# Order of the precomputed weight sums, and the place of one squaring, in a fused attention and MLP kernel

## The chip, the cores and the metric

The kernel runs on one core of a Trainium2 chip. The metric is device time in microseconds (us) of one execution. A core has a matrix engine (PE, with PEld for its weight loads), a vector engine (DVE), a scalar engine (ACT), a general engine (POOL) and a DMA issuer (SP). Each engine takes its own instructions strictly in program order; they meet through semaphores only.

## The reference, cut to what matters

```python
batch, n_heads, seq, head_dim = (8, 12, 448, 64)

def rmsnorm(x, g):
    rms = np.sqrt(np.mean(x * x, axis=-1, keepdims=True) + 1e-06)
    return x / rms * g
q_n, k_n = (rmsnorm(q, g_q), rmsnorm(k, g_k))
scores = scale * np.matmul(q_n, k_n.transpose(0, 1, 3, 2))
...
attn = np.exp(scores)
...
return np.matmul(attn, v)

# then, per batch: d_model 768, inner width 3072
xn = (x - mu) / np.sqrt(var + 1e-06) * g_ln
ch = np.maximum(xn @ w_ch1, 0.0) @ w_ch2
return x + ch
```

## The kernel before, in words

**Tiling.** Heads go in pairs, six pairs to a batch, 48 in all (pair numbers p). Pairs are prepared in units (u) of up to two pairs; from unit 4 on a unit is two pairs of one batch. For each pair the attention has seven steps (i = 0 to 6). In step i the code first emits whatever the preparation plan has put there, then `scores(p, i)` (L405, in step 6 L411 for both pairs at once; PE writes a block of scores into a PSUM bank `psS`, ACT takes exp of it into `E`, L421), then `values(p - 1, i)` (L458 and L460, products of the E of the pair before with the values; step 1 does two of them). There are two `psS` banks and a third one, so that a score block can be written when the exp three blocks back is done. After the last product of a pair `evac_o` (L473 to L480, DVE) divides by the row sums and frees `oA` and `oB`; the next pair's products need these.

**Two streams in one.** `run_rest` goes over the batches. The MLP of batch b is a list of chunks, and after each half chunk `upto` emits so many attention steps of batch b+1 that both end together. Batch 0 has its own form, `first_mlp`: up products, and then 24 down chunks (`psC`, L728), six banks of four chunks, each ended by an `add` (L755, DVE). In it the attention is done with the last 11 chunks still to go; after each of those one piece of the layer norm of batch 1 follows: statistics, `norm` of two token tiles (L662, DVE), and their transposes by DMA into `xnT` (L688, issued by SP).

**The MLP from batch 1 on** (`mlp_group`) multiplies two token tiles by w2 with seven block products instead of eight. Products take w2 itself or sums of its four blocks b11, b12, b21, b22: T1 = b12 - b11, T2 = b22 - T1, T4 = b21 - T2, and T3 = b12 - b22, which is written over b12. T1, T2 and T4 lie in `w2s`. Product "7" needs T3 after nine up chunks and product "1" of the first group; "6", "5" and "4" need T2, T1 and T4 later, "4" (T4) last. `weight_sums` (L761) makes each sum in four DVE subtractions of 1152 columns, T1, T2 and T4 of one quarter after one another, then those of the next; the four of T3 are in `last`. `run_rest` gives out one of these 16 subtractions after each chunk: in batch 0 when fewer than nine chunks are left (`left < 9`), the rest in batch 1, one a chunk from its first.

**The preparation of a unit** (`pieces`) is a set of lettered operations that `PLAN` puts into steps, counted from four pairs ahead of the unit's first pair: a, the square of the keys on ACT (L259, `khl<-k`); i, keys by the gains on POOL (L279); c, the square of the queries on ACT (L259, `qn<-q`), the first reader of the loaded queries; d and e, the row sums of the two squares on DVE (L265); j, the keys in fp16 on ACT (L287); k, their remainder on DVE (L290); g, the root (L268, L269); l, the scaled queries on DVE (L83); m, their copy; x, y, Y, transposes by DMA on SP. Units 10 to 24, fifteen of them, follow `PLAN`; here they are called steady units. The others have places of their own. The query buffer is one of a ring of three; when a k or an l has freed one, the load of a later unit goes into it (L146 and L154, SP), behind what SP has in its queue.

Of the kernel before, what the change touches and what calls it, by code (L numbers as in the profile page):

```python
# [51 lines left out]
NAMES = {8: ["bai", "d", "c", "e", "j", "k", "gz", "l", "m"],  # L52
         9: ["bai", "d", "c", "j", "k", "e", "gz", "l", "m"]}
W2_AT = 47, 71
PLAN = ((0, "bai"), (1, "dc"), (3, "j"), (5, "k"), (6, "e"), (7, "g"), (8, "l"), (9, "m"),
        (12, "z"), (15, "x"), (16, "y"), (18, "Y"))
LOAD_AT = 3, 1
LN_EXP_SET = 6
# [33 lines left out]
class _Fast:  # L92
# [447 lines left out]
    def attention(self):  # L540
# [3 lines left out]
        for u in range(4, nu):  # L544
            p, m = UNIT_PAIR[u], UNITS[u][2]
            if u == 4:
                continue
            plan = [(7 * (p - 4) + x, y) for x, y in PLAN]
            if u in EARLY:
# [208 lines left out]
    def weight_sums(self):  # L758

        nc, w2, w2s = self.nc, self.sh.w2, self.w2s  # L760
        sub = lambda out, a, b: nc.vector.tensor_tensor(out=out, in0=a, in1=b, op=ALU.subtract)  # L761
        ops = []
        for c in range(4):
            f, f2 = slice(3 * c, 3 * c + 3), slice(HALF + 3 * c, HALF + 3 * c + 3)
            b11, b12, b21, b22 = w2[:, f, 0:HCOL], w2[:, f, HCOL:DM], w2[:, f2, 0:HCOL], w2[:, f2, HCOL:DM]
            t1, t2, t4 = (w2s[:, i, f] for i in range(3))
            ops += [lambda a=a: sub(*a) for a in ((t1, b12, b11), (t2, b22, t1), (t4, b21, t2))]
        last = [lambda f=slice(3 * c, 3 * c + 3), f2=slice(HALF + 3 * c, HALF + 3 * c + 3): sub(
            w2[:, f, HCOL:DM], w2[:, f, HCOL:DM], w2[:, f2, HCOL:DM]) for c in range(4)]
        return ops, last  # L770

    def mlp_group(self, b, tiles, end, before=(), after=()):

# [186 lines left out]
    def upto(self, target):  # L960
        while self.pos < min(target, len(self.steps)):
            for call in self.steps[self.pos]:
                call()
            self.pos += 1
# [8 lines left out]
    def run_rest(self):  # L973
        steps, mark, upto = self.steps, self.mark, self.upto
        for b in range(B):
            tail = TAIL[b]
            chunks = list(self.mlp_chunks(b))
            total = sum(c for c, _ in chunks)
            if b + 1 == B:
                for i, (_, emit) in enumerate(chunks):  # L980
                    if i == len(chunks) - 55:
                        self.tc.mark_branch_hint_location("general", "LikelyTaken", [ENG.PE, ENG.DVE, ENG.SP, ENG.Activation, ENG.Pool])
                    for call in emit if isinstance(emit, list) else [emit]:
                        call()
                    if i in FLAG_AT:
                        self.flag(FLAG_AT.index(i))
                break
            start, goal = self.pos, mark[b + 1]
            done, items = 0.0, None
            if b == 0:  # L990
                ops, last = self.weight_sums()
            elif b == 1:
                ops += last
            left = sum(c > 0 for c, _ in chunks)
            for cost, emit in chunks:
                if not cost:
                    emit()
                    continue
                for i, call in enumerate(emit):
                    call()  # L1000
                    if i + 1 < len(emit):
                        upto(int(min(goal, start + (goal - start) * (done + cost / 2) / (total - 960 * tail))))
                left -= 1
                if (left < 9 if b == 0 else b == 1) and ops:
                    ops.pop(0)()
                done += cost
                upto(int(min(goal, start + (goal - start) * done / (total - 960 * tail))))
                if self.pos >= goal:
                    if items is None:
                        items = self.ln_list(b + 1)  # L1010
                        for u, (x, _, _) in enumerate(UNITS):
                            if x == b + 2 and self.late_v(u):
                                self.ln[f"Z{u}"] = self.prep_ops(u)["z"]
                                items.append(f"Z{u}")
                    if items and (items[0][0] != "X" or left <= DOWN):
                        x = items.pop(0)
                        self.ln[x]()
            for x in items:
                self.ln[x]()
            if b + 2 == B:  # L1020
                upto(len(steps))
# [223 lines left out]
```

## Time and profile before

| what | value |
|---|---|
| median of 3 runs | 586.15 us (585.71 to 586.3) |
| time of the profiled execution | 586.28 us |
| its span, first to last instruction | 584.7 us |
| DVE busy | 379.6 us (65%) |
| ACT busy | 376.9 us (64%) |
| POOL busy | 190.7 us (33%) |
| granted PE clock | 0.999 |

Times in the views of the profile count from the start of the span. The timeline has a line for each stretch of like instructions: start, length, engine, source line, operation, what it writes and reads, and in brackets how long the engine sat idle before it and what ended that. A list of waits says which engine waited for whom. The chain that ended last follows the work back from the last instruction. Rows of PE overlap by up to 0.2 us, since a matmul's stated end is that of its pipeline.

### The profile page before, as it was taken

What the parts mean: (1) busy time and instruction counts of PE and PEld (TensorE: products, weight loads), DVE (VectorE), ACT (ScalarE), POOL (GpSimd) and SP (SyncE); (2) the same over time, 40 slices, a digit from 0 to 9 for tenths busy, and PEclk for the clock granted to TensorE, in tenths of its full rate; (3) what the DMA queues carried; (4) which work ended last, traced back from release to release, by engine and by line L of the source; (5) the groups of instructions that cost most, each with busy time, mean ns of one, the idle gap of its engine ahead of it and who ended that gap; (6) DMA issues with size and microseconds to landing.
All of it is one profiled execution on the core that took longest, in us unless ns stands there. A gap on an engine that the chain in (4) does not pass through costs nothing.

```text
span 584.7 us, 13655 instructions
## 1 busy us (share of the span) xinstructions
PE 563.6 (96%) x5446; PEld 414.6 (71%) x5446; DVE 379.6 (65%) x826; ACT 376.9 (64%) x691; POOL 190.7 (33%) x207
## 2 busy tenths in 40 slices
PE   6888999999999999999999999999999999999996
PEld 5656666677686867777677767777777777777784
DVE  6989567799657566845667585854757634663424
ACT  4997887458784769557786588737787477323130
POOL 5885635303430710553240520643141410020000
PEclk9999999999999999999999999999999999999999
DMA  7999999948673966978563797958743490030201
GB/s 205 272 235 229 206 192 167 193 133 131 119 130 86 149 137 131 117 157 112 120 112 48 183 127 148 109 149 121 143 58 64 127 102 1 2 108 1 83 2 58
DMA packets 178329, 72.59 MB, mean 124 GB/s; under 512 B 138212, under 2 KB 173220, under 8 KB 178260
## 3 DMA queue, kind: packets, MB, share of 16 engines
q1 hardware_dynamic: 133876, 52.52, 43.3%
q0 software_dynamic: 43440, 18.52, 24.7%
q8 instruction: 44, 0.72, 0.5%
q10 hardware_dynamic: 944, 0.62, 0.4%
q14 instruction: 25, 0.20, 0.1%
HBM read 52.76 MB, written 11.01 MB: 109 GB/s over the span
## 4 chain that ended last, share of the span: by engine, by line
PE 70%; DMA 10%; DVE 8%; ACT 5%; SPq 2%; issue 2%; POOL 1%; DVEq 0%; ACTq 0%; POOLq 0%
PE psH L795 30%; PE psP L818 27%; PE psS L405 6%; PE oA L458 4%; DMA q<-in_q_dram 3%; ACT E L421 3%; DMA v<-in_v_dram 2%; DMA w2s<-in_k_dram 2%; SPq L154 2%; DVE w2s L761 1%; PE oB L460 1%; PE psS L411 1%; DVE ssq L265 1%; DVE qn L83 1%; DMA kU<-khl 1%
## 5 line engine op out<-in xcount | busy, mean ns | idle before, releaser
L421 ACT ACTIVATE E<-psS,rr_all 128x448 f16<-128x448 f32 x336 | 204.0, 636 | 39.7 <-PE psS L405 34.9
L795 PE MATMUL psH<-xnT,w 128*128 128x256 f16 (+1 forms) x2016 | 225.8, 261 | 0.0
L795 PEld LDWEIGHTS <-w 128*128 128x128 f16 x2016 | 172.7, 98 | 23.9 <-issue 4.7
L798 ACT ACTIVATE hS<-psH 128x512 f16<-128x512 f32 x150 | 90.0, 601 | 95.8 <-PE psH L795 91.5
L818 PEld LDWEIGHTS <-hS 128*128 128x128 f16 x1080 | 100.0, 98 | 57.5 <-issue 1.1
L818 PE MATMUL psP<-w,hS 128*128 128x384 f16 x672 | 126.8, 326 | 0.0
L405 PE MATMUL psS<-qU,kU 128*128 128x448 f16 x288 | 101.9, 356 | 6.1 <-ACT E L421 4.4
L458 PEld LDWEIGHTS <-E 128*128 128x128 f16 x1008 | 70.4, 98 | 39.5 <-issue 5.0
L279 POOL TENSOR_TENSOR k<-k,gprod 128x896 f32<-128x896 f32 x18 | 38.4, 2132 | 149.6 <-ACT khl L259 133.1
L801 DVE TENSOR_TENSOR hS<-hS 128x512 f16<-128x512 f16 (+1 forms) x119 | 56.7, 484 | 22.3 <-ACT hS L798 20.8
L818 PE MATMUL psP<-w2s,hS 128*128 128x384 f16 (+1 forms) x408 | 69.9, 321 | 0.0
L458 PE MATMUL oA<-v,E 128*128 128x65 f16 x864 | 67.2, 193 | 2.2 <-DVE x L475 1.4
L755 DVE SCALAR_TENSOR_TENSOR x<-psP,rs_all,x 128x384 f32<-128x384 f32 x60 | 36.4, 616 | 41.9 <-PE psP L818 41.2
L460 PE MATMUL oB<-v,E 128*128 128x65 f16 x288 | 52.0, 193 | 0.3
L829 POOL TENSOR_TENSOR x<-x,hS 128x384 f32<-128x384 f32 x21 | 23.5, 1129 | 83.5 <-ACT hS L897 82.9
L216 POOL DMA_DIRECT2D v<-in_v_dram x54 | 41.4, 777 | 9.9 <-PE oB L460 8.9
L473 DVE RECIPROCAL rec_all<-oA 128x6 f32<-128x6 f32 x48 | 9.2, 192 | 47.5 <-PE oA L458 47.4
L290 DVE TENSOR_TENSOR khl<-k,khl 128x896 f16<-128x896 f32 x18 | 19.6, 1089 | 28.8 <-ACT khl L287 27.6
L897 ACT ACTIVATE hS<-hS,rs_all 128x384 f32<-128x384 f32 x27 | 14.6, 604 | 33.1 <-DVE hS L801 33.1
L405 PEld LDWEIGHTS <-kU 128*128 128x128 f16 x288 | 28.2, 98 | 10.8 <-issue 2.1
L460 PEld LDWEIGHTS <-E 128*128 128x128 f16 x336 | 32.4, 97 | 0.5 <-DVE xl L480 0.5
L265 DVE TENSOR_REDUCE ssq<-khl 128x14 f32<-128x896 f32 (+1 forms) x24 | 25.5, 1061 | 5.0 <-ACT khl L259 4.8
(146 smaller groups left out, 628.3 us busy)
## 6 DMA issues: line engine op xcount, KB each, us to landing
k<-in_k_dram SPq DMA_DIRECT2D x19, 384.0 KB, 4.3
q<-in_q_dram SPq DMA_DIRECT2D x18, 384.0 KB, 4.1
out_dram<-x SPq DMA_DIRECT2D x14, 384.0 KB, 3.0
w<-in_moe_w_ch_dram POOLq DMA_DIRECT2D x3, 1536.0 KB, 13.6
v<-in_v_dram POOLq DMA_DIRECT2D x54, 64.0 KB, 4.6
out_dram<-x POOLq DMA_DIRECT2D x9, 384.0 KB, 2.7
w<-in_moe_w_ch_dram POOLq DMA_DIRECT2D x1, 2304.0 KB, 22.3
w<-in_moe_w_ch_dram POOLq DMA_DIRECT2D x2, 1152.0 KB, 14.2
```

What stands on the lines that cost most here:

```text
L216: nc.gpsimd.dma_start(out[:, :, j, 0:D], main[:, :, j])
L265: nc.vector.tensor_reduce(out=c["ssq"][:, n], in_=c["sq", n], axis=AX.X, op=ALU.add)
L279: (nc.vector if u in DVE_KG else nc.gpsimd).tensor_tensor(out=c["t"][1], in0=c["t"][1], in1=sh.gprod.unsqueeze(1).broadcast_to([128, g, D] ...
L405: nc.tensor.matmul(ps[0][:, 0:S], c["main"][:, ts(i, 128)], c["q"][:, ts(h, S)], start=True, stop=True)
L421: nc.scalar.activation(out=o, in_=x[:, 0:S], func=AFT.Exp, scale=self.units[u][3][:, g:g + 1], bias=EXP_BIAS)
L458: nc.tensor.matmul(oA[:, t, cs], E[:, ts(t, 128)], rhs, start=(i == 0 and t == 0), stop=(i == 6 and t == 2))
L460: nc.tensor.matmul(oB[:, cs], E[:, 320:448], rhs, start=(i == 0), stop=(i == 6))
L755: self.nc.vector.scalar_tensor_tensor(out=x, in0=ps, scalar=self.rs[:, b, t:t + 1], in1=x, op0=ALU.mult, op1=ALU.add)
L795: nc.tensor.matmul(ps[:, i], sh.w1[:, dc, ts(f + i, 128)], self.xnT[:, dc, 256 - N:256], start=(i == 0 and dc == 0), stop=(i == k - 1 and ...
L798: nc.scalar.activation(out=hT[:, f:f + k], in_=ps, func=AFT.Relu)
L801: nc.vector.tensor_tensor(out=out, in0=a, in1=c, op=op)
L818: nc.tensor.matmul(bank[x][:, c], a[:, f], w[:, f, c], start=(start and f == 0), stop=(stop and f == HALF - 1))
```

## The change

The diff has three edits. The first two belong together.

- `weight_sums` no longer puts the four T4 subtractions among those of T1 and T2; they come at the end of `last`, behind T3. So batch 0 gets eight subtractions (T1 and T2) where it had nine, and batch 1 eight (T3, then T4) where it had seven (the last T1, T2, T4, then T3).
- In batch 0 the first subtraction is given out one chunk sooner (`left < 10`).
- In `PLAN` the letter c moves from step 1 to step 2, for the fifteen steady units.

```diff
-PLAN = ((0, "bai"), (1, "dc"), (3, "j"), (5, "k"), (6, "e"), (7, "g"), (8, "l"), (9, "m"),
+PLAN = ((0, "bai"), (1, "d"), (2, "c"), (3, "j"), (5, "k"), (6, "e"), (7, "g"), (8, "l"), (9, "m"),
         (12, "z"), (15, "x"), (16, "y"), (18, "Y"))
...
-        ops = []
+        ops, t4s = [], []
...
-            ops += [lambda a=a: sub(*a) for a in ((t1, b12, b11), (t2, b22, t1), (t4, b21, t2))]
+            ops += [lambda a=a: sub(*a) for a in ((t1, b12, b11), (t2, b22, t1))]
+            t4s.append(lambda a=(t4, b21, t2): sub(*a))
...
-        return ops, last
+        return ops, last + t4s
...
-                if (left < 9 if b == 0 else b == 1) and ops:
+                if (left < 10 if b == 0 else b == 1) and ops:
```

No instruction is added or removed, and no operand changes.

## The prediction

> **What bounds the kernel now.** I read the page first, then PE's waits, first to 400 us and then from there, then the timeline of each engine around each wait.
>
> ```profile
> PE 563.6 (96%) x5446; PEld 414.6 (71%) x5446; DVE 379.6 (65%) x826; ACT 376.9 (64%) x691; POOL 190.7 (33%) x207
> ...
> PE psS L405 <- ACT E L421: 1.6, 2, 1.0
> PE oA L458 <- DVE x L475: 0.7, 1, 0.7
> ...
> PE oA L458 <- DVE x L475: 0.4, 1, 0.4
> ```
>
> PE bounds it. From 100 us on it waits four times, 1.6 + 0.7 + 0.4 = 2.7 us: two score blocks wait for an exp, two value products for an `evac_o`. The change removes no work, so it can win only what it takes out of these waits, and it loses where it makes PE wait anew. The last wait, at 497 us, lies behind the last steady unit and all weight sums; it stays.
>
> **The square: the first of two stalls.** ACT, PE and the chain of waits around 219 us:
>
> ```profile
> 218.62 0.95 ACT L259 ACTIVATE qn<-q 128x896 f32<-128x896 f32 x1 [2.32 <-DMA q<-in_q_dram]
> 219.48 1.14 ACT L421 ACTIVATE E<-psS,rr_all 128x448 f16<-128x448 f32 x2
> 220.51 0.60 ACT L798 ACTIVATE hS<-psH 128x512 f16<-128x512 f32 x1
> 220.99 0.96 ACT L287 ACTIVATE khl<-k 128x896 f16<-128x896 f32 x1
> 221.83 1.17 ACT L421 ACTIVATE E<-psS,rr_all 128x448 f16<-128x448 f32 x2
> ...
> 215.96 0.35 PE L405 MATMUL psS<-qU,kU 128*128 128x448 f16 x1
> ...
> 218.01 0.35 PE L405 MATMUL psS<-qU,kU 128*128 128x448 f16 x1
> ...
> 220.15 0.35 PE L405 MATMUL psS<-qU,kU 128*128 128x448 f16 x1 [1.01 <-ACT E L421]
> ...
> 221.11 0.35 PE L405 MATMUL psS<-qU,kU 128*128 128x448 f16 x1
> ...
> 222.52 0.91 PE L411 MATMUL psS<-qU,kU 128*64 128x448 f16 x4
> ...
> 214.64 3.96 DMA q<-in_q_dram
> ```
>
> The queries land at 214.64 + 3.96 = 218.60. The square c has stood at the head of ACT's queue since 216.3, and behind it stands the exp of step 1, whose scores were ready at 215.96 + 0.35 = 216.31. The two exps that begin at 219.48 are those of steps 1 and 2; the score block that waits, at 220.15, is step 4's, which needs the bank of step 1's exp. The pair's last block (222.52) is stretched too: it needs the banks of steps 3 and 4, whose exps begin at 221.83.
>
> With c in step 2 the order is exp 1, c, exp 2. Exp 1 runs at 216.34 in what is idle time now and its bank is free by 217.0, so step 4's block doesn't wait. But c still waits for the queries until 218.62; behind it come exp 2, the relu, j, exps 3 and 4, all without a pause. They move up by one exp alone: 219.48 + 1.14 is the end of two, and one takes 0.64 by itself, so 1.14 - 0.64 = 0.50 to 0.52. Exp 2 ends near 220.12, and step 5's block, which would come at 221.11 - 1.01 = 220.10, hardly waits; step 6's first bank comes free at 221.30 + 0.64 = 221.94, where PE would stand at 222.52 - 1.01 = 221.5. So what is late next is exp 3 and 4, and PE ends up earlier by the shift of ACT's queue, **0.52**, and not by 1.01. Bounds: nothing, if PE meets another wait before ACT has caught up; and the wait plus the stretch of the last block (0.91 against 0.57 in an undisturbed pair, a row below), 1.01 + 0.34 = 1.35. I take 0.52, since the queue behind c is in the rows without a gap.
>
> **The second stall** has the same build:
>
> ```profile
> 352.74 0.95 ACT L259 ACTIVATE qn<-q 128x896 f32<-128x896 f32 x1 [1.86 <-DMA q<-in_q_dram]
> 353.60 1.14 ACT L421 ACTIVATE E<-psS,rr_all 128x448 f16<-128x448 f32 x2
> ...
> 354.27 0.35 PE L405 MATMUL psS<-qU,kU 128*128 128x448 f16 x1 [0.55 <-ACT E L421]
> ```
>
> Here PE waits 0.55, and ACT's queue moves up by the same exp: 0.52, bounds 0 and 0.55 + 0.34 = 0.89.
>
> **The other thirteen steady units** show no idle of ACT ahead of c. There c and exp 1 change places, and exp 2 and all behind it begin when they do now, as long as exp 1's scores are there by the time c starts now. This is a tight one:
>
> ```profile
> 202.56 0.96 ACT L259 ACTIVATE qn<-q 128x896 f32<-128x896 f32 x1
> 203.40 1.17 ACT L421 ACTIVATE E<-psS,rr_all 128x448 f16<-128x448 f32 x2
> ...
> 205.75 1.19 ACT L421 ACTIVATE E<-psS,rr_all 128x448 f16<-128x448 f32 x2
> ...
> 201.79 0.35 PE L405 MATMUL psS<-qU,kU 128*128 128x448 f16 x1
> ...
> 207.08 0.57 PE L411 MATMUL psS<-qU,kU 128*64 128x448 f16 x4
> ```
>
> Exp 1's scores are there at 201.79 + 0.35 = 202.14, before c starts at 202.56: a pure exchange. I cost it at nothing. The cover is thin, though: exps 3 and 4 end at 205.75 + 1.19 = 206.94, and the second half of the block at 207.08 needs the latter's bank at about 207.36 less pipeline, some 0.34 later. If exp 4 came a whole square (0.95) later, PE would lose 0.95 - 0.34 = 0.6 here. What reads the square is the row sum e in step 6, four steps on; c itself issues nothing else, and passes no DMA: y of the unit before is in the same step, but on SP.
>
> **The weight sums.** DVE, PE, SP and POOL around the end of batch 0's MLP:
>
> ```profile
> 110.99 1.88 DVE L662 SCALAR_TENSOR_TENSOR xn<-x,stat,gln 128x768 f16<-128x768 f32 x2
> ...
> 113.43 0.75 DVE L761 TENSOR_TENSOR w2s<-w 128x1152 f16<-128x1152 f16 x1
> ...
> 130.37 0.75 DVE L761 TENSOR_TENSOR w<-w 128x1152 f16<-128x1152 f16 x1
> ...
> 131.46 0.56 DVE L475 TENSOR_TENSOR x<-oA,rec_all 128x384 f32<-128x384 f32 x1
> ...
> 132.38 2.23 DVE L761 TENSOR_TENSOR w<-w 128x1152 f16<-128x1152 f16 x1
> ...
> 134.86 1.07 DVE L265 TENSOR_REDUCE ssq<-khl 128x14 f32<-128x896 f32 x1
> ...
> 111.00:131.00 20.00, 20.00 (x174) 14.99 (x172) 19.83 (x32) 8.52 (x19) 1.44 (x3) 1.00 0.71 150
> ...
> L761 DVEq EVENT_SEMAPHORE  x3: 21/21/50, 111.0 to 111.2; - x3
> ...
> 118.57 1.47 PE L795 MATMUL psH<-xnT,w 128*128 128x256 f16 x12
> ...
> 131.00 0.35 PE L405 MATMUL psS<-qU,kU 128*128 128x448 f16 x1
> 132.07 0.27 PE L458 MATMUL oA<-v,E 128*128 128x65 f16 x3 [0.72 <-DVE x L475]
> ...
> 114.00 2.57 SPq L688 DMA_TRANSPOSE xnT<-xn  x2
> ...
> 131.90 2.09 POOL L279 TENSOR_TENSOR k<-k,gprod 128x896 f32<-128x896 f32 x1 [19.46 <-ACT khl L259]
> ```
>
> From 111 to 131 us DVE is busy 19.83 of 20 us: a queue, where each subtraction pushes all behind it by its 0.75. Now 15 subtractions stand ahead of the `evac_o` that ends at 131.46 + 0.56 = 132.02 and lets PE go at 132.07. After the change batch 0 gives eight and the first six chunks of batch 1 six: **14 ahead of it**. So DVE frees `oA` 0.67 to 0.75 sooner (0.75, less the overlap with its neighbour), and PE, which stands there since 131.35, waits next to nothing: 0.67 to 0.72 gained.
>
> The sixteenth subtraction, now a T4, comes back after the eighth chunk, ahead of the row sum at 134.86. From there on DVE is where it is now, or up to some 0.4 later, since POOL's product (131.90 to 133.99) starts by ACT's squaring of the keys, which can move up only by some 0.3. Who waits for that row sum:
>
> ```profile
> 136.03 0.95 ACT L287 ACTIVATE khl<-k 128x896 f16<-128x896 f32 x1
> ...
> 138.25 1.17 ACT L421 ACTIVATE E<-psS,rr_all 128x448 f16<-128x448 f32 x2
> ...
> 139.67 0.57 PE L411 MATMUL psS<-qU,kU 128*64 128x448 f16 x4
> ```
>
> j at 136.03 overwrites what the row sum reads, and follows its end (134.86 + 1.07 = 135.93). Behind j in ACT's queue lie the exps up to 138.25 + 0.64 = 138.89, whose bank the second half of the block at 139.67 needs. PE, 0.7 earlier, would be there at about 139.2: 0.3 to spare with j where it is, 0.1 to 0.45 lost with j 0.4 to 0.75 later. So the term is 0.72 less 0.1, **0.6**, bounds 0.25 and 0.72.
>
> The earlier start costs nothing that I find. The first subtraction now comes after the first of the two norms at 110.99; its semaphores were passed at 111.2. The second norm then ends at 113.6 instead of 112.87, and SP, busy with what is ahead in its queue, issues its transpose as the second of the two from 114.00, at 115.3. PE's first use of it, at 118.57, stays. T3, made sooner, is ready before product "7"; T4, last, is wanted last.
>
> The Trainium skill ("SBUF — State Buffer", section "Who interferes with whom") says that a vector instruction with two inputs in SBUF and a GpSimd instruction that reads SBUF exclude one another for the whole instruction, whichever came first. The 2.23 us subtraction of the fence above agrees: begun at 132.38, it ended 0.62 after POOL's product did. By that rule the exchange of T3 for T4 in that place changes nothing, and the added sixteenth would be held only if POOL began after it.
>
> **Sum.** 0.52 + 0.52 + 0.6 = 1.64, so 586.28 - 1.64 = 584.64 for the profiled execution (its span is 584.7, 1.6 lies around it). That execution is 0.13 above the median of the runs, so 584.5 against 586.15. All four waits lie on PE, which has no idle between them to take the gain up again.
>
> **The rivals.** What a measurement of this kernel can tell from no change is about 0.2%, 1.17 us.
>
> 1. *Only one part works.* Either the gain at 132 is given back at 139, because DVE's queue is not lighter when j's row sum comes (for it: one subtraction stands right ahead of that row sum; against: the 0.3 of slack), which leaves 1.04 and gives 585.1; or the squares bring nothing and the sums do, 585.5.
> 2. *Nothing moves:* PE earlier by fractions meets the next late exp or landing each time. 586.1. Against it: no other PE wait over 0.1 is in the list.
> 3. *The stalls go whole:* queries that land sooner, because SP issues their load after fewer delays, would free 1.35 and 0.89 as well as 0.72: 586.15 - 2.96 = 583.2. For it speaks only that SP's queue follows DVE and PE.
> 4. *Slower:* in the steady units exp 2 to 4 come a whole square later, because exp 1 cannot use the place that c leaves (its scores not yet there). Four units have only some 0.34 of slack (the one above, its twin a period of 134 us later, and the unit after each): 4 x 0.6 = 2.4 lost, the two stalls unchanged, the sums' 0.6 won: 586.15 + 1.8 = 588.0. It decides from a delay of exp 4 by 0.34 on. Against it: 202.14 before 202.56.
>
> **How the numbers follow.** My forecast 0.56 (0.04 of it within 0.2%, since its own range, from 0.25 + 0.4 + 0.4 to 0.72 + 0.6 + 0.6 won, is 584.2 to 585.1), rival 1 0.17, rival 2 0.06, rival 3 0.08, rival 4 0.13. Faster by over 0.2%: 0.52 + 0.08 = 0.60. Within: 0.17 + 0.06 + 0.04 = 0.27. Slower: 0.13. The range takes in rivals 1 and 2 and most of the way to 3, and leaves out 4 and the end of 3: 583.5 to 586.3.
>
> **What would show it.** Right: no wait of PE near 132 us; step 4's block without a wait in the two units, exp 1 ahead of c, c still waiting for its queries, and the last block of the pair stretched more than now; the last T4 ahead of the row sum near 134.9, j no later than 136.5. Wrong: c without a wait in those units (rival 3); a PE wait near 139 as long as the one lost at 132 (rival 1); new waits of `psS` for exp at 206, 237 and 340 us (rival 4); the first product of batch 1 later than 118.6.

## The result, and the profile after

| | median, us | runs |
|---|---|---|
| before | 586.10 (584.05 to 586.61) | 22 |
| changed | 584.73 (583.19 to 586.91) | 22 |

The ratio is 0.998, with a 95% interval of 0.9972 to 0.9988: 1.2 us faster, between 0.7 and 1.6 (the two medians alone differ by 1.37). Two further comparisons on other occasions gave 0.9987 (0.9971 to 1.0003) and 0.9959 (0.9948 to 0.9971). The forecast was 584.5, 1.65 us faster.

The profiled execution of the changed kernel took 584.28 us, its span is 582.7. Its page and PE's waits from 100 us on (who waited for whom, us in total, times, longest):

```profile
PE 563.3 (97%) x5446; PEld 414.2 (71%) x5446; DVE 379.9 (65%) x826; ACT 376.0 (65%) x691; POOL 190.4 (33%) x207
...
PE psS L411 <- ACT E L421: 0.7, 2, 0.5
PE oA L458 <- DVE x L475: 0.4, 1, 0.4
PE psH L796 <- DMA xnT<-xn: 0.4, 1, 0.4
```

The wait for an eviction at 132 us is gone, and so is each wait of a step's single block (L405) for its exp. What remains of the two stalls sits at the pair's last block (L411), as forecast. A wait is new: 0.4 for the transposed tokens, at the start of batch 1. The changed kernel has one source line more, so L795 to L801 of before are L796 to L802 here.

**Around 132 us.** DVE, PE, POOL and ACT:

```profile
130.56 0.56 DVE L475 TENSOR_TENSOR x<-oA,rec_all 128x384 f32<-128x384 f32 x1
...
131.48 0.76 DVE L761 TENSOR_TENSOR w2s<-w,w2s 128x1152 f16<-128x1152 f16 x1
132.15 2.32 DVE L802 TENSOR_TENSOR hS<-hS 128x512 f16<-128x512 f16 x1
134.39 0.74 DVE L761 TENSOR_TENSOR w2s<-w,w2s 128x1152 f16<-128x1152 f16 x1
135.06 1.07 DVE L265 TENSOR_REDUCE ssq<-khl 128x14 f32<-128x896 f32 x1
...
131.71 0.25 PE L458 MATMUL oA<-v,E 128*128 128x65 f16 x3
...
132.08 2.11 POOL L279 TENSOR_TENSOR k<-k,gprod 128x896 f32<-128x896 f32 x1 [19.63 <-ACT khl L259]
...
136.23 0.95 ACT L287 ACTIVATE khl<-k 128x896 f16<-128x896 f32 x1 [0.88 <-DVE ssq L265]
```

The eviction ends at 131.12 instead of 132.02, PE comes at 131.71 and finds `oA` free. The instruction held by POOL's product is another one now: the subtraction at 131.48 got through ahead of it, and the 0.41 us sum behind (L802) took 2.32, up to 0.28 after the product's end at 134.19. In e7, a second profile of the changed kernel, the product was held too: it began at 131.53, 0.09 behind a subtraction, and took 2.61 instead of 2.1. The last T4 follows at 134.39, the row sum at 135.06 (134.86 before), and j at 136.23.

**Around 219 us.** ACT and PE:

```profile
215.16 1.31 ACT L421 ACTIVATE E<-psS,rr_all 128x448 f16<-128x448 f32 x2 [0.53 <-PE psS L405]
217.65 0.95 ACT L259 ACTIVATE qn<-q 128x896 f32<-128x896 f32 x1 [1.18 <-DMA q<-in_q_dram]
218.51 0.62 ACT L421 ACTIVATE E<-psS,rr_all 128x448 f16<-128x448 f32 x1
...
220.34 1.16 ACT L421 ACTIVATE E<-psS,rr_all 128x448 f16<-128x448 f32 x2
...
221.03 0.91 PE L411 MATMUL psS<-qU,kU 128*64 128x448 f16 x4 [0.24 <-ACT E L421]
```

Exps 0 and 1 now stand ahead of the square, one exp alone right behind it. The square still waits for its queries, and the last block for exp 3.

### The profile page after: what moved, and what is told of

The parts are those of the page before. It is cut to its first block, busy times and chain, and to the rows that moved or that the text cites. A ratio compares the mean times of both kernels' runs of the same rounds, so it can differ in the third digit from the quotient of the medians.

```text
span 582.7 us, 13655 instructions
## 1 busy us (share of the span) xinstructions
PE 563.3 (97%) x5446; PEld 414.2 (71%) x5446; DVE 379.9 (65%) x826; ACT 376.0 (65%) x691; POOL 190.4 (33%) x207
## 4 chain that ended last, share of the span: by engine, by line
PE 78%; DVE 7%; DMA 5%; ACT 5%; issue 2%; SPq 2%; ACTq 0%; DVEq 0%
PE psH L796 32%; PE psP L819 28%; PE psS L405 7%; PE oA L458 4%; ACT E L421 3%; PE psH L718 2%; DMA q<-in_q_dram 2%; DMA w2s<-in_k_dram 1%; PE oB L460 1%; PE psS L411 1%; DVE ssq L265 1%; DVE stat L641 1%; DMA k<-in_k_dram 1%; ACT khl L259 1%; SPq L154 1%
## 5 line engine op out<-in xcount | busy, mean ns | idle before, releaser
L796 PE MATMUL psH<-xnT,w 128*128 128x256 f16 (+1 forms) x2016 | 225.8, 261 | 0.4 <-DMA xnT<-xn 0.4
L796 PEld LDWEIGHTS <-w 128*128 128x128 f16 x2016 | 172.6, 98 | 24.5 <-issue 4.7
L405 PE MATMUL psS<-qU,kU 128*128 128x448 f16 x288 | 101.4, 354 | 5.1 <-ACT E L421 3.3
L802 DVE TENSOR_TENSOR hS<-hS 128x512 f16<-128x512 f16 (+1 forms) x119 | 58.7, 500 | 22.3 <-ACT hS L799 20.8
L290 DVE TENSOR_TENSOR khl<-k,khl 128x896 f16<-128x896 f32 x18 | 19.6, 1088 | 29.4 <-ACT khl L287 29.4
L405 PEld LDWEIGHTS <-kU 128*128 128x128 f16 x288 | 28.1, 98 | 11.1 <-issue 2.4
```

The costliest lines, as they stand in the source:

```text
L405: nc.tensor.matmul(ps[0][:, 0:S], c["main"][:, ts(i, 128)], c["q"][:, ts(h, S)], start=True, stop=True)
L796: nc.tensor.matmul(ps[:, i], sh.w1[:, dc, ts(f + i, 128)], self.xnT[:, dc, 256 - N:256], start=(i == 0 and dc == 0), stop=(i == k - 1 and ...
L802: nc.vector.tensor_tensor(out=out, in0=a, in1=c, op=op)
```

## The experiments

Each was timed beside runs of the kernel before on the same chip; the median of before stands once for those that shared it.

| | median, us | before | ratio (95% interval) |
|---|---|---|---|
| e1 square alone | 585.00 | 585.85 | 0.9987 (0.9977 to 0.9997) |
| e2 sums alone | 585.04 | | 0.9983 (0.9974 to 0.9992) |
| e3 T4 behind T3 alone | 585.14 | | 0.9988 (0.9977 to 0.9999) |
| e4 earlier start alone | 587.06 | | 1.0016 (1.0000 to 1.0031) |
| e5 square in step 3 | 585.12 | 586.03 | 0.9983 (0.9974 to 0.9992) |
| e6 square in step 4 | 584.71 | | 0.9983 (0.9973 to 0.9994) |
| e7 changed, again | 584.43 | | 0.9987 (0.9971 to 1.0003) |
| e9 step 4 for two units | 583.42 | 586.12 | 0.9964 (0.9952 to 0.9975) |
| e10 step 3 for two units | 584.28 | | 0.9970 (0.9958 to 0.9982) |
| e11 changed, no earlier start | 584.01 | | 0.9971 (0.9962 to 0.9980) |
| e12 changed, third time | 583.68 | | 0.9959 (0.9948 to 0.9971) |

e8 is a second profile of the kernel before, with one time, 586.37. Executions scatter by some 1 us either way, as much as the whole change, so most of what follows is read from the profiles. A profile shows one execution: those of e9 and e10 were the fastest of their 10 and 7, that of e12 the slowest of its 6. PE's program is the same in all of them, 5446 instructions in one order, so the start of the same instruction can be set side by side. The places are the first product of batch 1, the first up product after the pair that ends near 140 us, the score block of step 1 and the first up product after the last block in unit 14, and the same two in unit 20 (starts from the timelines, us).

| profile | batch 1 | 140 | unit 14 | after | unit 20 | after | span |
|---|---|---|---|---|---|---|---|
| before | 118.57 | 140.17 | 215.96 | 223.36 | 350.53 | 357.48 | 584.7 |
| e8 before again | 119.34 | 140.94 | 216.72 | 224.14 | 351.31 | 358.11 | 584.8 |
| e1 | 118.92 | 140.04 | 215.93 | 222.81 | 350.09 | 356.24 | 583.6 |
| e2 | 119.58 | 140.04 | 215.82 | 222.92 | 350.08 | 356.96 | 583.8 |
| e3 | 118.34 | 139.33 | 215.10 | 222.48 | 349.64 | 356.22 | 583.6 |
| e4 | 118.81 | 141.02 | 216.79 | 223.96 | 351.12 | 358.04 | 585.8 |
| changed | 119.10 | 139.57 | 215.45 | 221.87 | 349.13 | 355.90 | 582.7 |
| e7 changed | 118.55 | 139.41 | 215.29 | 221.06 | 348.33 | 354.58 | 582.2 |
| e12 changed | 120.13 | 140.59 | 216.47 | 222.96 | 350.22 | 356.29 | 583.6 |
| e11 | 118.75 | 139.76 | 215.65 | 221.42 | 348.69 | 355.08 | 582.1 |
| e5 | 118.88 | 139.74 | 216.31 | 222.25 | 350.20 | 356.14 | 583.9 |
| e6 | 118.48 | 140.16 | 215.90 | 221.84 | 349.36 | 355.30 | 582.4 |
| e9 | 118.51 | 139.36 | 215.25 | 221.19 | 348.45 | 354.39 | 581.6 |
| e10 | 118.35 | 139.22 | 215.10 | 221.04 | 348.32 | 354.26 | 581.1 |

**e1, the square alone.**

```diff
-PLAN = ((0, "bai"), (1, "dc"), (3, "j"), ...
+PLAN = ((0, "bai"), (1, "d"), (2, "c"), (3, "j"), ...
```

> The square one step later, the sums as before. Theory (each of the two stalls gives back one exp, 0.5 us, changed by how early the queries land): PE wait near 132 us stays at 0.7, the batch 1 start stays without a wait, about 0.5 us gained near 219 and 0.5 near 353 with 0.5 of scatter each, 1.0 us faster in all. Rival (stalls go whole once the exp is ahead of the square): 2.2 us faster. Rival (the two parts need one another): no gain.

Measured: 0.9987. PE's waits:

```profile
PE oA L458 <- DVE x L475: 0.6, 2, 0.4
PE psS L411 <- ACT E L421: 0.5, 1, 0.5
PE psH L795 <- DMA xnT<-xn: 0.3, 1, 0.3
```

From the block of step 1 to the product after the pair, unit 14 takes 222.81 - 215.93 = 6.88 where it took 7.40, and unit 20 takes 6.15 for 6.95: 0.52 and 0.80 won. The wait near 132 is there but only 0.2 long (0.6 less the 0.4 at 497), since PE itself came late: this kernel waits for `xnT` too, with the weight sums untouched. So the new wait at the start of batch 1 needs none of the sums' edits.

**e2, the sums alone, and e3, T4 behind T3 without the earlier start.** e2 is the changed kernel with c back in step 1; e3 besides

```diff
-                if (left < 10 if b == 0 else b == 1) and ops:
+                if (left < 9 if b == 0 else b == 1) and ops:
```

> T4 behind T3 and the first subtraction one piece sooner, the square as before. Theory: the PE wait of 0.72 near 132 us goes, the two stalls for an exp near 219 and 353 stay at about 1.0 and 0.55, about 0.6 us faster. If the late start of batch 1 in the changed kernel (PE waits 0.35 for xnT at 119.1) comes from the second norm standing behind the first subtraction, it is here again and 0.5 of the gain is lost; if it is scatter of the DMA issuer's queue, it comes and goes, with the same lateness of the transposes issued before 110 us.

> T4 behind T3 without the earlier start (batch 0 gives eight subtractions in its last nine chunks but one), the square as before. Theory (the count of subtractions ahead of the eviction near 131 us decides, and it is 14 here too): the same gain as with the earlier start, 0.6 us. Rival (the earlier start is what helps): no gain. If the norm behind the first subtraction delays batch 1, this kernel starts batch 1 by up to 0.35 us earlier than the one with the earlier start.

Measured: 0.9983 and 0.9988, no difference between them. The waits of e2, then of e3:

```profile
PE psS L405 <- ACT E L421: 1.2, 2, 0.7
PE psH L796 <- DMA xnT<-xn: 0.8, 1, 0.8
PE oA L458 <- DVE x L475: 0.4, 1, 0.4
```

```profile
PE psS L405 <- ACT E L421: 1.2, 2, 1.0
PE oA L458 <- DVE x L475: 0.4, 1, 0.4
```

Both lose the wait near 132 (the 0.4 left is the one at 497) and keep both stalls. e3 has its eviction as early as the changed kernel (131.12 both), so the order does most of it, not the earlier start; what the earlier start adds is told under e4 and e11. That e2 starts batch 1 at 119.58 and e3 at 118.34 looks like the norm behind the first subtraction; e7, e9, e11 and e12 below tell that it isn't.

**e4, the earlier start alone.**

```diff
-                if (left < 9 if b == 0 else b == 1) and ops:
+                if (left < 10 if b == 0 else b == 1) and ops:
```

> The first subtraction one piece sooner, T4 where it was: ten subtractions in batch 0, and 16 instead of 15 ahead of the eviction near 131 us. Theory: that eviction comes 0.7 us later and the PE wait near 132 grows from 0.72 to about 1.4; 0.7 us slower than before. Rival (the earlier start helps by itself): 0.3 to 0.7 us faster.

Measured: 1.0016 (1.0000 to 1.0031), slower, by an interval that begins at no change. The waits, a root on ACT, and DVE's eviction:

```profile
PE psS L405 <- ACT E L421: 1.3, 2, 0.8
PE oA L458 <- DVE x L475: 1.1, 2, 0.7
PE psH L795 <- ACT hS L798: 0.4, 1, 0.4
...
127.81 0.23 ACT L268 ACTIVATE rt<-ssq 128x28 f32<-128x28 f32 x1 [3.12 <-DVE ssq L265]
...
132.31 0.56 DVE L475 TENSOR_TENSOR x<-oA,rec_all 128x384 f32<-128x384 f32 x1
```

With 16 subtractions ahead the eviction ends at 132.87; with 15 it was 132.02 before, with 14 it is 131.12 in the changed kernel. These ends move from profile to profile (131.89 to 132.79 with 15, 130.88 to 131.87 with 14), since the whole queue begins earlier or later. Counted from the start of the first norm near 111 us they are sharp: 21.83 us with 16, 21.03 to 21.05 with 15 (three profiles), 20.37 with 14 and without the earlier start (e3, e11), 20.11 or 20.12 with 14 and the earlier start (six profiles; e2 and e12, whose batch 1 starts latest of these, have 20.31 and 20.38). So one subtraction less is worth 0.67. The rest is the order within the queue, as three subtractions of e3 on DVE show, T1, T2 and the next T1:

```profile
113.19 0.75 DVE L761 TENSOR_TENSOR w2s<-w 128x1152 f16<-128x1152 f16 x1
113.97 0.76 DVE L761 TENSOR_TENSOR w2s<-w,w2s 128x1152 f16<-128x1152 f16 x1
114.65 0.75 DVE L761 TENSOR_TENSOR w2s<-w 128x1152 f16<-128x1152 f16 x1
```

T2 reads the T1 ahead of it and starts 0.78 after it; the next T1 reads nothing of T2 and starts 0.68 after it. Four subtractions ahead of the eviction stand right behind one that they read before and in e3, five in e4, two in e7, where the earlier start pairs them otherwise. With 0.11 for each, 20.37 becomes 20.15 (measured 20.12), and 21.04 + 0.67 + 0.11 = 21.82 (measured 21.83).

The wait did not grow to 1.4, though: PE came later itself, 0.4 of it at a wait for a relu (the last line of the list), which stood on ACT behind a root that idled 3.12 us for a row sum out of the same queue of DVE. The product near 140 us is 0.85 later than before (141.02).

**e5 and e6, a still later square.** The changed kernel with

```diff
-PLAN = ((0, "bai"), (1, "d"), (2, "c"), (3, "j"), ...
+PLAN = ((0, "bai"), (1, "d"), (3, "cj"), ...          (e5)
+PLAN = ((0, "bai"), (1, "d"), (3, "j"), (4, "c"), ... (e6)
```

> The changed kernel with the square of the queries in step 3, ahead of the keys' fp16 copy. Theory (in the two stalled units what waits behind the square counts, and the square itself no longer waits once two exps and a relu are ahead of it): the remaining waits of the pair's last block near 221 and 355 us, 0.24 and 0.49 plus the stretch, go to 0.1 or less; 0.9 us faster than the changed kernel, 2.1 faster than before. Rival (the later square pushes exps 3 and 4 in the tight units): waits for exp of 0.3 to 0.6 appear near 206, 237, 340 and 371 us, and it is no faster than the changed kernel.

> The changed kernel with the square of the queries in step 4, behind the keys' fp16 copy and exp 3. Theory: the square does not wait for its queries at all, the two stalls go, 1.0 us faster than the changed kernel, about the same as with step 3. Rival: the row sum in step 6 comes too close, the root and the scaled queries and with them the transposes of the unit are later, and it is slower than with step 3.

Measured: 0.9983 both, no faster than the changed kernel beside them: a miss. The waits of both stalls do go, in e5 and e6 alike: 5.94 us instead of 7.40 in unit 14, 5.94 instead of 6.95 in unit 20, 1.46 and 1.01 won. (The last block takes 0.74 there; where it takes an undisturbed 0.57, in e7 and e11, unit 14 takes 5.77.) The gain goes elsewhere. From 140 us to unit 14 e5 takes 76.57 us and the changed kernel 75.88, from the end of that pair to unit 20 again 0.69 more. ACT of e5 in unit 13:

```profile
203.98 0.60 ACT L799 ACTIVATE hS<-psH 128x512 f16<-128x512 f32 x1 [0.16 <-PE psH L796]
204.47 0.94 ACT L259 ACTIVATE qn<-q 128x896 f32<-128x896 f32 x1
205.31 0.94 ACT L287 ACTIVATE khl<-k 128x896 f16<-128x896 f32 x1
206.15 2.72 ACT L421 ACTIVATE E<-psS,rr_all 128x448 f16<-128x448 f32 x5
```

Square and copy now stand back to back behind a relu, and the exps after them start at 206.15, where they started at 205.75 before. PE's list shows no wait for it; PE loses it in bits of 0.1 to 0.3, one of them near 186 us, where its weight loads wait 0.8 for DVE (the place is shown under "The other thirteen units" below). In e6 the first place is unit 10; ACT and PE:

```profile
136.10 0.95 ACT L287 ACTIVATE khl<-k 128x896 f16<-128x896 f32 x1 [1.15 <-DVE ssq L265]
...
138.32 0.96 ACT L259 ACTIVATE qn<-q 128x896 f32<-128x896 f32 x1
139.16 2.22 ACT L421 ACTIVATE E<-psS,rr_all 128x448 f16<-128x448 f32 x4
...
139.85 0.38 PE L411 MATMUL psS<-qU,kU 128*64 128x448 f16 x2 [0.81 <-ACT E L421]
```

j waits there for the late row sum, the square comes behind it, and exp 4 behind both: 0.81 lost in one block. Two more are units 15 and 21: from the product after the pair before to that after theirs e6 takes 15.02 and 15.03 us, where it was 14.60. This is the rival of the prediction that ends slower, at work one and two steps further on.

**e7, e12: the changed kernel again; e8: the kernel before again.**

> The changed kernel once more, beside the two with a still later square, for a second profile. Theory: 1.2 us faster than before; no wait near 132; the waits near 219 and 353 again about 0.4 to 0.6 each, whichever of the two is larger; the wait for xnT at the start of batch 1 between 0 and 0.5, as late as the transposes of unit 9 are.

> The changed kernel a third time, for its profile and for the comparison with the three above. Theory: 1.2 us faster than before; each of the two stalls shrinks by 0.5 from where the landing of its queries would put it; in three profiles the sum of both gains lies between 0.8 and 2.4.

> The kernel before once more, for a second profile of it. Theory: waits of 0.7 near 132, 1.0 and 0.55 near 219 and 353, each with the scatter of the landing of the queries, 0.3 to 0.5; the first product of batch 1 at 118.6 where the transposes of unit 9 are as early as in the first profile, later where they are late.

e8 has its waits as expected, but not its start of batch 1: 119.34, though unit 9's key transpose ended sooner than before (107.43 against 108.41). PE doesn't wait there; this execution is already 0.76 behind near 106 us (an add on DVE starts at 106.70, before at 105.94). In e7 nothing but the last wait, 0.4 near 497, is in the list, so the waits of 0.4 to 0.6 that were expected at both stalls are not; e12 waits 0.9 for `xnT`:

```profile
PE psH L796 <- DMA xnT<-xn: 0.9, 1, 0.9
PE oA L458 <- DVE x L475: 0.4, 1, 0.4
PE psS L411 <- ACT E L421: 0.3, 1, 0.3
```

SP tells both starts of batch 1 apart. First e7, then e12 (the issue of unit 9's key transpose, then those of the two token tiles, on SP):

```profile
101.58 6.88 SPq L306 DMA_TRANSPOSE kU<-khl  x1
...
114.06 2.58 SPq L688 DMA_TRANSPOSE xnT<-xn  x2
```

```profile
102.53 7.38 SPq L306 DMA_TRANSPOSE kU<-khl  x1
...
115.86 2.55 SPq L688 DMA_TRANSPOSE xnT<-xn  x2
```

The token tiles follow the end of unit 9's key transpose (108.46 and 109.91) by 5.6 and 5.95 us; it was 5.6 before (108.41, 114.00). Both belong to the same kernel. That key transpose lies ahead of everything the change touches, so the late start is scatter of SP's queue. Before, the late eviction could cover up to 0.7 of it (in e1, 0.33 late for `xnT`, the wait near 132 is 0.24); now nothing does.

The two stalls can be put in one line. Let W be the time from the start of step 1's block on PE to the start of the square on ACT, that is, to the landing of the queries:

| profile | W, unit 14 | won | W, unit 20 | won |
|---|---|---|---|---|
| before | 2.66 | - | 2.21 | - |
| e8 | 2.69 | -0.02 | 2.06 | 0.15 |
| e2 | 2.37 | 0.30 | 2.15 | 0.07 |
| e3 | 2.65 | 0.02 | 1.85 | 0.37 |
| e4 | 2.43 | 0.23 | 2.18 | 0.03 |
| e1 | 2.67 | 0.52 | 1.94 | 0.80 |
| changed | 2.20 | 0.98 | 2.56 | 0.18 |
| e12 | 2.28 | 0.91 | 1.86 | 0.88 |
| e7 | 1.43 | 1.63 | 2.04 | 0.70 |
| e11 | 1.50 | 1.63 | 2.17 | 0.56 |

With c in step 1 (upper five) the gain is what W is shorter than before: 2.66 - 2.37 = 0.29 for 0.30. With c in step 2 (lower five) it is 0.52 more than that: 0.52 + 2.66 - 2.20 = 0.98 for 0.98, and 0.52 + 2.21 - 2.56 = 0.17 for 0.18, up to where the stall is gone. Why W is shorter in unit 14 in all four profiles with both edits (1.43 to 2.28, without both 2.37 to 2.69) is open. It is not one thing: in e7 SP has issued the load 1.54 us ahead of step 1's block, where it was 0.72 before; in e11 it is issued as late as before (0.77 ahead), but the square starts 2.27 after that instead of 3.38.

**e9 and e10, a late square for units 14 and 20 alone.**

```diff
             plan = [(7 * (p - 4) + x, y) for x, y in PLAN]
+            if u in (14, 20):
+                plan = [(at + 2 * (y == "c"), y) for at, y in plan]   # e10: 1 instead of 2
```

> The changed kernel with the square of the queries in step 4 for units 14 and 20 alone, the two whose queries land late; the other thirteen keep step 2. Theory (step 3 and 4 won the whole of both stalls, 1.5 and 1.0 us against before, and gave it back in the tight units): both stalls gone, no wait near 140, 236 and 370, 0.8 us faster than the changed kernel, 2.3 faster than before in the profile. Rival (what step 4 lost elsewhere comes from the two units' later roots and transposes): waits behind 225 and 360 us, no gain.

> The same with step 3, ahead of the keys' fp16 copy, for units 14 and 20 alone. Theory: both stalls gone as well, the same 0.8 us. Rival (the square ahead of the copy pushes exps 3 and 4): a wait of 0.2 to 0.5 at the last block of one of the two pairs.

ACT of e9 in unit 14, and PE's waits:

```profile
217.99 0.94 ACT L287 ACTIVATE khl<-k 128x896 f16<-128x896 f32 x1
218.83 0.63 ACT L421 ACTIVATE E<-psS,rr_all 128x448 f16<-128x448 f32 x1
219.35 0.95 ACT L259 ACTIVATE qn<-q 128x896 f32<-128x896 f32 x1
...
PE oA L458 <- DVE x L475: 0.4, 1, 0.4
```

The square no longer waits, the waits of both stalls are gone (5.94 us in each unit, in both kernels), and nothing is lost elsewhere against the changed kernel: spans of 581.6 and 581.1, the shortest of all, though of fast executions. In the times the 0.8 that was expected doesn't show: they can't be told from the changed kernel beside them (0.9964 and 0.9970 against 0.9959). Against the four profiles with step 2 the late square wins between -0.2 and 0.8 in a unit, less than the scatter.

**e11, the changed kernel without the earlier start.** The edit is that of e3.

> The changed kernel without the earlier start of the subtractions. Theory (the earlier start does nothing, the count of 14 does it all): no wait near 132, the first product of batch 1 follows the second transpose, which comes 7.0 us after the issue of unit 9's key transpose has ended, with or without the earlier start; the same time as the changed kernel. Rival: the norm no longer behind a subtraction starts batch 1 up to 0.5 us sooner.

Measured: 0.9971, no difference from the changed kernel beside it. Batch 1 starts at 118.75 without a wait; so it does with the earlier start in e7 and e9 (118.55, 118.51). In the times the earlier start is neither of use nor of harm. In the profiles it is of some use: PE's value product near 131 us starts 0.42 after its score block in e3 and e11, 0.19 in e7 and e9 (1.07 before), and the stretch from batch 1's first product to the one near 140 is 20.99 and 21.01 without it, 20.85 to 20.87 with it (e5, e7, e9, e10). That is 0.14, less than a comparison of times can tell.

## Why the prediction was right

**The sums.** Forecast 0.6, bounds 0.25 and 0.72. The stretch from batch 1's first product to the one near 140 us took 21.60 us before and takes 20.86 in e7, 20.85 in e9, 20.99 in e3: 0.6 to 0.75 won. The count of subtractions ahead of the eviction was the right reason: one less is worth 0.67, e3 shows it without the earlier start, and e4 shows the reverse with one more. The forecast gave nothing to the earlier start, which brought the eviction 0.25 forward, and PE 0.14 of it. The last T4's price came out as forecast: row sum 0.2 later, j at 136.23 with 136.5 as its limit, no wait at 139. The text had the subtraction in the old place held as before; in the changed kernel and e7 it got through, and the sum behind it was held, while in e3 and e11 it was the subtraction (2.54 us). And its clause that the sixteenth "would be held only if POOL began after it" has the order the wrong way round: in each of these cases the one that was held began after POOL's product. The rule on shared reads from the Trainium skill ("SBUF — State Buffer", section "Who interferes with whom") fits these profiles, that of e7 too, where POOL's product came second: first come, first served, and the second held to the end.

**The start of batch 1.** "The earlier start costs nothing that I find" holds, e3 against e2 and e11 against e12 show no difference in time. One sign of being wrong did show, "the first product of batch 1 later than 118.6": it came at 119.10. As a sign it was worth little, since the kernel before has 119.34 in e8. But the place was thinner than the text had it: the second transpose reaches PE with little to spare, and a late key transpose of unit 9 makes PE wait 0.3 to 0.9, with the edit (e2, e12) and without it (e1).

**The stalls.** Forecast 0.52 each, because ACT's queue moves up by one exp and the square waits as before. e1 shows it bare in unit 14, 0.52 at an unchanged W. In the changed kernel's own profile the terms are 0.98 and 0.18, since W was 0.46 shorter and 0.35 longer: "c still waits for the queries until 218.62" took the landing for fixed. That the sum, 1.16, was hardly off 1.04 is luck: in e7, e11 and e12 it is 2.33, 2.19 and 1.79. The mechanism, one exp, is what e1 and the table of W show.

**The other thirteen units** were costed at nothing. They cost some 0.3: near 186, 320 and 453 us PE loses 0.1 each time, in every profile with c in step 2 (in the table above, 140 us to unit 14: 75.89 in e1 and 75.88 in the changed kernel, 75.79 before, 75.78 in e2), and not in e2 and e3. The text asked for exp 1's scores to be there when c starts, and looked at one unit. In units 12, 18 and 24 they weren't. Unit 12 on ACT and DVE before:

```profile
171.81 0.94 ACT L259 ACTIVATE qn<-q 128x896 f32<-128x896 f32 x1
173.10 0.64 ACT L421 ACTIVATE E<-psS,rr_all 128x448 f16<-128x448 f32 x1 [0.35 <-PE psS L405]
...
177.09 1.09 DVE L290 TENSOR_TENSOR khl<-k,khl 128x896 f16<-128x896 f32 x1 [3.22 <-ACT khl L287]
```

The same in the changed kernel, and who waited from 183 to 190 us (PEld is PE's weight load):

```profile
173.89 0.94 ACT L259 ACTIVATE qn<-q 128x896 f32<-128x896 f32 x1
...
177.09 1.09 DVE L290 TENSOR_TENSOR khl<-k,khl 128x896 f16<-128x896 f32 x1 [3.83 <-ACT khl L287]
...
PEld L819 <- DVE hS L802: 0.5, 2, 0.3
```

Before, c ran while exp 1 had to wait for its scores anyway. Behind exp 1 it no longer fills that gap; j and then k (L290) come no sooner than before, though PE is 0.6 ahead by then. DVE goes on from k without a pause to the sums that PE's weights are loaded from, and two weight loads wait for them, 0.5 in all, of which PE loses 0.1. Each profile with c in step 2 has this wait at all three places, and none with c in step 1 has it.

**The sum.** The changed kernel's profile is 2.0 us shorter than that of before. To the product near 140 us it has won 0.60, to unit 14 lost 0.09, in unit 14 won 0.98, on the way to unit 20 lost 0.09, in unit 20 won 0.18: 1.58 at 355.90, and 1.48 after the 0.1 near 453. The remaining 0.5 lies at the end, behind 490 us; two profiles of the kernel before differ by 0.5 there (e8 is 0.63 behind at 358.11 and 0.1 at the end), so it is scatter. The 22 runs gained 1.2, less than the 1.65 of the forecast. Two things that it put at nothing, the 0.3 of the three units and a wait of up to 0.9 at the start of batch 1, go in that direction; that they are the whole difference is not shown.

**The rivals.** That only one part works (1) is out: e1 and e2 win by themselves, and no wait near 139 has come. So is that nothing moves (2). That the stalls go whole (3) came true in part, in e7 and e11 for unit 14, where the queries landed soon enough; unit 20 shows no such profile. The slower one (4) had the right mechanism for units 12, 18 and 24, at 0.1 each; its larger losses need a square that comes a step later still.

## What to carry to other kernels

Where an engine's queue waits for a load, put ahead of it all that is ready: moving the load's first reader back by one place wins one place, and the full wait only once enough stands ahead of it; but move back just the instance that is late, for the others can pay for it (three units here, more in e5 and e6), and before calling an exchange free check in each instance that the one moved ahead is ready. In a backed-up queue count the instructions ahead of the one that another engine waits for: work that is wanted last belongs behind it. When the queue starts matters little, but an instruction right behind the one whose result it reads costs a little more than one that isn't.

## What the runs showed of the hardware

The issue of one DMA transpose (unit 9's keys) ended anywhere from 106.9 us (e11: 101.57 and 5.29) to 109.9 (e12) in kernels that don't differ up to there; it took between 5.27 (e8) and 7.58 us (e1). The landing of the queries of unit 14, seen from PE, moved by 0.85 within three profiles of the changed kernel (W of 1.43 to 2.28). Such scatter is as large as this change, and a single profile shows it as a gain or a loss of the edit.

A subtraction of 0.75 us on DVE was followed by the next after 0.66 to 0.68 us, and after 0.78 or 0.79 where the next reads its result (e3, e7). Where a two-input instruction on DVE and POOL's product overlapped, the one that began later took longer: on DVE 2.2 to 2.5 us instead of 0.4 or 0.75 (before, changed, e3), on POOL 2.61 instead of 2.1 (e7).
